# Attention into two expert layers on one core: query tiles by token halves, a rank for each operation of a pair in the scheduler, and constant matmuls over the whole array

## The chip, the cores and the metric

One Trainium2 (trn2) chip, one of its cores. The metric is the device time of one execution in microseconds. The kernel before was timed three times: 1214.74 us median, 1212.67 to 1214.76 us. Engines are called as the profile calls them: PE (TensorE), DVE (VectorE), ACT (ScalarE), POOL (GpSimd), SP (the engine that issues the DMAs). PEld is PE's weight load.

## The reference, cut to what matters

Two batches of 8 heads, 576 tokens, head size 64. Each head adds two attentions: one over keys and values averaged in groups of 4 tokens (144 x 144), its rows repeated 4 times, and one in which a token sees only the keys less than 4 places away. The result, 1152 tokens by 512, goes through two layers of experts (8 and 4 experts, hidden size 1024), each expert computed for every token and weighted.

```python
out_d = sm_attn(q_d, k_d, v_d)              # q_d, k_d, v_d: means over 4 tokens
out_up = np.repeat(out_d, factor, axis=2)   # factor = 4
mask = np.abs(pos[:, None] - pos[None, :]) < factor
scores = np.where(mask, scale * q @ k.T, -1e9)
out_local = softmax(scores) @ v
x = out_up + out_local
for e in range(E):                          # E = 8, then the same with E = 4
    h = np.maximum(x @ w1[e], 0.0)
    out += P[:, e:e + 1] * (h @ w2[e])
```

## The kernel before, in words

**Pairs of heads.** The attention runs over 8 pairs of heads (the loop over `i` at the end of the first plan). A pair fills the partitions: one head on 0 to 63, the other on 64 to 127. For the local attention the 576 queries are cut into 10 tiles of 58 (`QT`; the last has 54), each against a window of 64 keys (`win`). `scores` (L578) computes them in two halves of 5 tiles: a mask matmul (L587), then 10 small matmuls (L594). DVE takes the maximum (L605) and subtracts it (L607), ACT takes the exponential (L612), `norm` sums and inverts on DVE and multiplies on POOL (L622) into `pn`. `pool_qk` and `pool_v` form the averages on POOL; `pooled` (L660) gives the 144 x 144 scores `ed`, which POOL (L686) and ACT (L691) normalise.

**Turning and values.** `turn_scores` (L695) transposes on PE: four blocks of `pn` (L704), then the fifth block and `ed` (L713). Two neighbouring tiles `2t, 2t+1` go through one transpose, so after it the even tiles lie on partitions 0 to 63 and the odd ones on 64 to 127. `values` multiplies them with the values (L749, 20 matmuls) into two banks, one for the even and one for the odd tiles, and the averaged values (L739) into the first. ACT repeats each averaged row 4 times into `od` (L757, 128x576); DVE adds both (L764), taking every second tile of `xs` in each of its two calls. `halves` splits `xs` into two parts `xh` and `xl` (L776, L778), which the expert layers multiply separately.

**What follows.** When the pairs 0 to 3 are done, the tokens of batch 0 are complete, and 8 `plain_unit`s of 12 matmuls (L263) for expert 0 can run beside the pairs 4 to 7. Four tiles of its second product follow (L441, 48 matmuls of 512 columns). Then comes a second plan: gate logits (L901), the same for batch 1, sums of `xh` and `xl` (`x_sums`: POOL L850, DVE L855 and L867), and the expert loop, whose matmuls are L382 and L441.

**The order.** A planner (`Plan`) decides it when the program is built. Each task has an engine, a cost in ns, and a due time, which is PE's planned clock when the task was added plus `slack` plus `bias`. `run` takes the tasks in simulated time: on each engine, of the first `LOOK` tasks by due time, the one that can begin first by the planned costs, ties going to the earlier due time. The result is a fixed list for each engine, so an instruction that waits holds up everything behind it on its engine. Buffers come from rings (`r_pn` has 2, PE's result banks 8).

**Constant matmuls.** `warm_up` (L495) issues matmuls of constants into a free bank, whose result nobody reads: 28 at the start, 12 after the first scores, and up to 16 wherever the planner sees PE idle for over 0.3 us. They load one column of ones (128x1) and stream 128 columns.

```python
    def warm_up(b, n):
        for _ in range(n):
            nc.tensor.matmul(out=b[0:1, 384:512], lhsT=one, rhs=row)
```

Of the kernel before, what the change touches and what calls it, by code (L numbers as in the profile page):

```python
# [78 lines left out]
class Plan:  # L79
# [7 lines left out]
    def __init__(self):  # L87
        self.tasks, self.last, self.readers = [], {}, {}
        self.clock, self.later, self.bias = 0.0, [], 0.0

    def add(self, eng, cost, fn, reads=(), writes=(), slack=0.0, after=None):
# [98 lines left out]
def tile_attention_moe_moe(  # L190
# [22 lines left out]
    QT = W - 6  # L213
    NQ = -(-S // QT)
    SD = S // 4
    HD = SD // 2
# [266 lines left out]
    r_sm, r_ed = ring(4, "sm", [128, NQ, W + 1]), ring(4, "ed", [HD, 4, SD + 1])  # L483
    r_pn = ring(2, "pn", [128, NQ, W])
# [7 lines left out]
    one = nc.const_aps.tensor(1.0, [128, 1], BF16)  # L492
    row = nc.const_aps.tensor(1.0, [128, 128], BF16)

    def warm_up(b, n):  # L495

        for _ in range(n):
            nc.tensor.matmul(out=b[0:1, 384:512], lhsT=one, rhs=row)  # L498

    def win(t):  # L500
        return min(max(QT * t - 3, 0), S - W)

    def queries(t):
        return min(QT, S - QT * t)

# [7 lines left out]
    for j, t in enumerate((0, 1, NQ - 1)):  # L513
        off = win(t) - QT * t

# [12 lines left out]
    for mx in r_mxd.slots:  # L528
        nc.vector.memset(mx[:, :, 1], -scale / 16.0)
    for od in r_od.slots:  # L530
        nc.vector.memset(od[:, S:], 0.0)
    nc.vector.tensor_copy(out=mask[:, 0, :], in_=mask_f[:, 0, :])
# [45 lines left out]
    def scores(i):  # L578

        s = st[i]  # L580
        for h, (lo, hi) in enumerate(HALVES):
# [3 lines left out]
            def mm(lo=lo, hi=hi, n=n, ps=ps):  # L585
# [5 lines left out]
                for t in range(lo, hi):  # L591
                    for y in range(2):
                        p0 = 64 * y
                        nc.tensor.matmul(  # L594
                            out=ps.slot[p0:p0 + queries(t), (t - lo) * W:(t - lo + 1) * W],
                            lhsT=x[p0:p0 + 64, 0, QT * t:QT * t + queries(t)],
                            rhs=x[p0:p0 + 64, 1, win(t):win(t) + W],
                            start=False, stop=(t == hi - 1),
                        )
# [15 lines left out]
    def norm(i):  # L615
# [6 lines left out]
        plan.add("POOL", 1300.0, lambda: nc.gpsimd.tensor_tensor(  # L622
            out=s["pn"].slot, in0=s["sm"].slot[:, :, 0:W],
            in1=s["su"].slot[:, 0:NQ].unsqueeze(2).to_broadcast([128, NQ, W]), op=ALU.mult), (su, *sm), (s["pn"],))

# [69 lines left out]
    def turn_scores(i):  # L695

        s = st[i]
        for j, (lo, hi, x) in enumerate(((0, 4, None), (4, 5, 0), (5, 5, 1))):
            ps = r_bank.new()
            n = 128 * (hi - lo)  # L700

            def mm(ps=ps, lo=lo, hi=hi, x=x, n=n):
                for t in range(lo, hi):
                    nc.tensor.transpose(  # L704
                        ps.slot[:, (t - lo) * 128:(t - lo + 1) * 128],
                        s["pn"].slot[:, 2 * t:2 * t + 2, :].rearrange("p t w -> p (t w)"), ident,
                    )
# [10 lines left out]
            keys = ((s["pn"],) if n else ()) + (((s["ed"], 2 * x), (s["ed"], 2 * x + 1)) if x is not None else ())  # L718
            plan.add("PE", 0.9 * n + (260 if x is not None else 0) + 80, mm, keys, (ps,))
            if n:  # L720
# [8 lines left out]
    def values(i):  # L729
        s = st[i]  # L730

        o = [r_bank.new() for _ in range(2)]
        E = NQ // 2 * QT

        def pooled_values():
            for kt in range(2):
                for x in range(2):
                    p0 = 64 * x
                    nc.tensor.matmul(  # L739
                        out=o[0].slot[p0:p0 + 64, E:E + SD], lhsT=s["vd"].slot[:, 2 * kt + x, :],  # L740
                        rhs=s["adT"].slot[:, x, kt, :], start=(kt == 0), stop=(kt == 1),
                    )

        def local(lo, hi):
            for t in range(lo, hi):
                for x in range(2):
                    for e in range(2):
                        p0, e0 = 64 * x, 64 * e
                        nc.tensor.matmul(  # L749
                            out=o[e].slot[p0:p0 + 64, QT * t:QT * t + QT],  # L750
                            lhsT=s["vw"].slot[e0:e0 + 64, t, p0:p0 + 64],
                            rhs=s["aT"].slot[e0:e0 + 64, t, p0:p0 + QT],
                        )

        plan.add("PE", 600.0, pooled_values, (s["vd"], (s["adT"], 0), (s["adT"], 1)), ((o[0], "d"),))

        plan.add("ACT", 650.0, lambda: nc.scalar.activation(  # L757
            out=s["od"].slot[:, 0:S].rearrange("p (t r) -> p t r", r=4),
            in_=o[0].slot[:, E:E + SD].unsqueeze(2).to_broadcast([128, SD, 4]),
            func=ACTF.Copy, scale=0.25), ((o[0], "d"),), (s["od"],))  # L760
        plan.add("PE", 16 * 60.0, lambda: local(0, 4), (s["vw"], (s["aT"], 0)), ((o[0], "l"), (o[1], "l")))
        plan.add("PE", 4 * 60.0, lambda: local(4, NQ // 2), (s["vw"], (s["aT"], 1)), ((o[0], "l"), (o[1], "l")))
        for e in range(2):
            plan.add("DVE", 170 + E, lambda e=e: nc.vector.tensor_tensor(  # L764
                out=s["xs"].slot.rearrange("p (t e q) -> p t e q", e=2, q=QT)[:, :, e],
                in0=o[e].slot[:, 0:E].rearrange("p (t q) -> p t q", q=QT),
                in1=s["od"].slot.rearrange("p (t e q) -> p t e q", e=2, q=QT)[:, :, e],
                op=ALU.add), ((o[e], "l"), s["od"]), ((s["xs"], e),))

    def halves(i):  # L770
# [6 lines left out]
                 xs, (("xh", i),))  # L777
        plan.add("DVE", 850.0, lambda: nc.vector.tensor_tensor(  # L778
            out=lo, in0=s["xs"].slot[:, 0:S], in1=hi.bitcast(F32), op=ALU.subtract),
# [5 lines left out]
    def warm(n):  # L785
        ps = r_bank.new()
        plan.add("PE", 60.0 * n, lambda: warm_up(ps.slot, n), (), (ps,))

    for i in range(NPAIR):
        pool_qk(i)  # L790
        scores(i)
# [6 lines left out]
        values(i)  # L798
        halves(i)

        if i == HP - 1:
# [272 lines left out]
def _layout(inputs):  # L1074
# [14 lines left out]
    for t in range(NQ):  # L1089
        s = min(max(QT * t - 3, 0), S - W)  # L1090
        vw[:, t % 2, :, t // 2] = vp[:, :, s:s + W].transpose(0, 2, 1, 3)
    v4 = vp.reshape(P, 2, 2, 72, 4, D).transpose(0, 3, 2, 1, 4, 5)
# [48 lines left out]
```

## Time and profile before

| | us |
|---|---|
| median of 3 timed runs | 1214.74 |
| the profiled execution, whole | 1222.66 |
| its span | 1220.9 |
| PE busy | 1213.9 (99%) |
| POOL busy | 679.5 (56%) |
| DVE busy | 665.0 (54%) |
| ACT busy | 463.4 (38%) |

The profiled execution is 7.92 us (0.65%) longer than the median. A stretch of the trace is named by its start and end in us from the span's start. The TensorE clock has two levels, 1.2 and 2.4 GHz; a granted clock of 0.50 is the lower, 1.00 the upper. Attention lies in the first 81 us, the four tiles of L441 behind it end at 91.92, where the logits begin.

### The profile page before, as it was taken

The numbers are of one execution on the slowest core, as the hardware profiler recorded it, in microseconds if no ns is written. First come the engines' busy times: TensorE is split into PE (matmuls) and PEld (weight loads), VectorE is DVE, ScalarE is ACT, GpSimd is POOL, SyncE is SP. The second block draws the span as 40 slices with busy tenths as digits, with TensorE's granted clock in tenths as the row PEclk, the third lists the DMA queues.
The fourth block names the chain that finished last, engine by engine and source line by source line (L and its number), as shares of the span: only waits on it lengthen the run. The fifth ranks groups of instructions, "written<-read, shape, count | busy, mean of one in ns | idle before, by whom it ended". The sixth has DMA issues, their size and how long they took to land.

```text
span 1220.9 us, 20041 instructions
## 1 busy us (share of the span) xinstructions
PE 1213.9 (99%) x7757; PEld 1088.3 (89%) x7757; DVE 665.0 (54%) x1202; ACT 463.4 (38%) x1155; POOL 679.5 (56%) x779
## 2 busy tenths in 40 slices
PE   9999999999999999999999999999999999999998
PEld 7788988989989989989889889899898898898997
DVE  7678846536536446446356356367453563653643
ACT  5565543513414414325325235144452251351430
POOL 7768835736637537438448357266383583573620
PEclk8699999999999999999999999999999999999999
DMA  8420201201202102102111112011021121120102
GB/s 239 127 78 10 96 35 36 69 26 45 69 1 70 53 18 69 45 26 70 38 33 70 35 35 70 32 56 35 18 70 35 35 70 35 36 69 20 34 1 77
DMA packets 27343, 63.71 MB, mean 52 GB/s; under 512 B 4528, under 2 KB 5296, under 8 KB 27248
## 3 DMA queue, kind: packets, MB, share of 16 engines
q1 hardware_dynamic: 27248, 62.44, 16.0%
q8 instruction: 60, 0.98, 0.3%
q14 instruction: 35, 0.29, 0.1%
HBM read 60.07 MB, written 2.36 MB: 51 GB/s over the span
## 4 chain that ended last, share of the span: by engine, by line
PE 96%; DVE 2%; DMA 1%; POOL 1%; issue 0%; ACT 0%; SPq 0%; POOLq 0%; DVEq 0%
PE bank L441 49%; PE bank L382 39%; PE bank L263 4%; PE bank L594 1%; DMA v<-in_v_dram 1%; PE bank L498 1%; PE bank L739 0%; PE bank L749 0%; PE bank L704 0%; DVE ht L352 0%; PE bank L901 0%; PE bank L713 0%; PE bank L877 0%; DVE tmp L392 0%; PE bank L587 0%
## 5 line engine op out<-in xcount | busy, mean ns | idle before, releaser
L441 PE MATMUL bank<-w2s,ht 128*128 128x512 f32 (+1 forms) x2604 | 602.8, 392 | 0.0
L441 PEld LDWEIGHTS bank<-w2s,ht 128*128 128x128 f32 x2604 | 485.1, 188 | 105.9
L289 POOL TENSOR_TENSOR w2s<-raw,w2s 128x512 fp32r<-128x512 f32 x96 | 133.2, 1399 | 396.5 <-PE bank L441 359.9
L469 DVE SCALAR_TENSOR_TENSOR acc<-bank,prob,acc 128x512 f32<-128x512 f32 (+1 forms) x190 | 142.2, 748 | 332.1 <-PE bank L441 332.1
L382 PE MATMUL bank<-sh,w1s 128*128 128x288 f32 x1408 | 294.3, 295 | 0.3 <-DVE tmp L392 0.3
L382 PEld LDWEIGHTS bank<-sh,w1s 128*128 128x128 f32 x1408 | 230.7, 188 | 0.5 <-DVE tmp L392 0.5
L382 PE MATMUL bank<-xh,w1s 128*128 128x288 f32 x1056 | 228.2, 295 | 0.1
L392 DVE TENSOR_TENSOR tmp<-bank,tmp 128x288 f32<-128x288 f32 x352 | 153.2, 450 | 119.2 <-ACT w1s L287 91.7
L352 DVE SCALAR_TENSOR_TENSOR ht<-tmp,ht 128x288 fp32r<-128x288 f32 x264 | 212.4, 831 | 4.4 <-ACT ht L350 1.3
L382 PE MATMUL bank<-sl,w1s 128*128 128x288 f32 x704 | 207.7, 295 | 0.0
L287 ACT ACTIVATE w2s<-raw 128x512 fp32r<-128x512 f32 x96 | 59.7, 624 | 378.8 <-PE bank L441 372.6
L382 PEld LDWEIGHTS bank<-xh,w1s 128*128 128x128 f32 x1056 | 175.6, 188 | 1.2 <-DVE tmp L392 0.4
L382 PE MATMUL bank<-xl,w1s 128*128 128x288 f32 x528 | 156.0, 295 | 0.0
L289 POOL TENSOR_TENSOR w1s<-t,w1s 128x256 fp32r<-128x256 f32 x176 | 141.7, 806 | 12.6 <-PE bank L382 6.6
L350 ACT ACTIVATE ht<-tmp 128x288 fp32r<-128x288 f32 x264 | 111.8, 444 | 88.5 <-DVE tmp L392 87.5
L289 POOL TENSOR_TENSOR w1s<-raw,w1s 128x256 fp32r<-128x256 f32 x148 | 120.5, 815 | 34.7 <-ACT w1s L287 33.7
L382 PEld LDWEIGHTS bank<-sl,w1s 128*128 128x128 f32 x704 | 132.2, 188 | 0.0
L382 PEld LDWEIGHTS bank<-xl,w1s 128*128 128x128 f32 x528 | 99.1, 188 | 0.9
L280 ACT ACTIVATE tmp<-bank 128x288 f32<-128x288 f32 x176 | 69.9, 408 | 64.2 <-PE bank L382 60.6
L352 DVE SCALAR_TENSOR_TENSOR ht<-bank,ht 128x288 fp32r<-128x288 f32 x120 | 54.4, 456 | 52.4 <-ACT ht L350 52.0
L313 POOL TENSOR_TENSOR t<-raw,t 128x256 f32<-128x256 f32 x88 | 80.8, 919 | 3.1
L287 ACT ACTIVATE w1s<-t 128x256 fp32r<-128x256 f32 x176 | 72.1, 410 | 17.8 <-POOL t L313 16.3
(113 smaller groups left out, 862.7 us busy)
## 6 DMA issues: line engine op xcount, KB each, us to landing
raw<-in_w1a_dram SPq DMA_DIRECT2D x32, 512.0 KB, 3.4
raw<-in_w2a_dram SPq DMA_DIRECT2D x64, 256.0 KB, 3.5
raw<-in_w1b_dram SPq DMA_DIRECT2D x16, 512.0 KB, 3.5
raw<-in_w2b_dram SPq DMA_DIRECT2D x32, 256.0 KB, 3.6
qk<-in_qk_dram SPq DMA_DIRECT2D x7, 576.0 KB, 6.3
vw<-in_vw_dram SPq DMA_DIRECT2D x8, 320.0 KB, 7.0
v<-in_v_dram SPq DMA_DIRECT2D x8, 288.0 KB
out_dram<-acc SPq DMA_DIRECT2D x8, 256.0 KB, 2.0
```

Of the source, the lines that this page charges most:

```text
L263: nc.tensor.matmul(out=ps[:, 0:U], lhsT=w[:, j, a:a + 128], rhs=b[:, k, c:c + U], start=(k == 0 and p == 0), stop=(k == HP - 1 and p == 2),)
L280: nc.scalar.activation(out=dst(), in_=src(), func=ACTF.Copy, **kw)
L287: plan.add("ACT", copy_cost(n), lambda: nc.scalar.activation(out=b.slot[:, 0], in_=src(), func=ACTF.Copy), (key,), ((b, 0),))
L289: plan.add("POOL", pool_cost(n), lambda: nc.gpsimd.tensor_tensor(out=b.slot[:, 1], in0=src(), in1=b.slot[:, 0].bitcast(F32), op=ALU.subtract),
L313: plan.add("POOL", pool_cost(256), lambda: nc.gpsimd.tensor_tensor(out=t.slot, in0=x(), in1=y(), op=ALU.subtract), (kx, ky), (t,))
L350: plan.add("ACT", c0[0], lambda: nc.scalar.activation(out=ht[:, s, 0, c:c + U], in_=src(), func=ACTF.Relu), (key,), ((*k, 0),))
L352: plan.add("DVE", c0[1], lambda: nc.vector.scalar_tensor_tensor(out=ht[:, s, 1, c:c + U], in0=src(), scalar=0.0, in1=ht[:, s, 0, c:c + U]. ...
L382: nc.tensor.matmul(out=o, lhsT=w.slot[:, j, 128 * k:128 * k + 128], rhs=a, start=(first and k == 0 and n == 0), stop=(k == 1 and n == 2), ...
L392: plan.add("DVE", cost, lambda: nc.vector.tensor_tensor(out=dst.slot, in0=ps.slot[:, 0:U], in1=b.slot, op=ALU.add), (ps, b), (dst,))
L441: nc.tensor.matmul(out=ps.slot[:, 0:nd], lhsT=ht[:, j, a, 128 * n:128 * n + 128], rhs=w[j].slot[:, b, c0:c0 + nd], start=(j == 0 and p == ...
L469: plan.add("DVE", 130 + 1.2 * nd, lambda: nc.vector.scalar_tensor_tensor(out=a, in0=ps.slot[:, 0:nd], scalar=prob[:, n, e:e + 1], in1=a, o ...
L498: nc.tensor.matmul(out=b[0:1, 384:512], lhsT=one, rhs=row)
```

## The change

1. **Tiles by halves of the tokens.** Tile `t` now begins at `288*(t // 5) + 58*(t % 5)`: five tiles in the first 288 tokens (58, 58, 58, 58, 56), five in the second. One transpose takes tile `j` of both halves, so the even/odd banks of `values` become first half and second half; `xs` is written in one piece for each, and the averaged rows are no longer repeated by ACT (`od` is 128x144) but read four times by DVE's add. Counts of instructions stay the same; one 54-query tile becomes two of 56. The layout of `vw` follows, done before the kernel.
2. **Ranks.** Each of the 42 operations that a pair adds gets its own offset (-37.8 to +30.0 us) on its due time, the same for all 8 pairs. The planner's cost for `xl` rises from 850 to 1200 ns, that for `od` falls from 650 to 300.
3. **Constants over the whole array.** `warm_up` now loads 128x128 ones, and six such matmuls stand at the head of each of the two `pn` transposes of the pairs 0 to 4 (60 in all). The planner sees less idle time on PE, so that of the constants that it fills in itself (16 at the start, then 16, 9 and 8) only the first 16 remain.

```diff
     def add(self, eng, cost, fn, reads=(), writes=(), slack=0.0, after=None):
         n = len(self.tasks)
+        if self.step is not None:
+            slack += self.ranks[self.step]
+            self.step += 1
...
-    r_od, r_xs = ring(2, "od", [128, NQ * QT]), ring(2, "xs", [128, NQ * QT])
+    r_od, r_xs = ring(2, "od", [128, SD]), ring(2, "xs", [128, S])
...
-            nc.tensor.matmul(out=b[0:1, 384:512], lhsT=one, rhs=row)
+            nc.tensor.matmul(out=b[:, 0:128], lhsT=row, rhs=row)
...
+    def begin(t):
+        return U * (t // NJ) + QT * (t % NJ)
...
-            out=s["pn"].slot, in0=s["sm"].slot[:, :, 0:W],
+            out=s["pn"].slot.rearrange("p j e w -> p e j w"),
+            in0=s["sm"].slot[:, :, 0:W].rearrange("p (e j) w -> p e j w", e=2),
...
+            w = 6 if i <= HP and j < 2 else 0
-            def mm(ps=ps, lo=lo, hi=hi, x=x, n=n):
+            def mm(ps=ps, lo=lo, hi=hi, x=x, n=n, w=w):
+                warm_up(ps.slot, w)
                 for t in range(lo, hi):
                     nc.tensor.transpose(
...
-        plan.add("ACT", 650.0, lambda: nc.scalar.activation(
-            out=s["od"].slot[:, 0:S].rearrange("p (t r) -> p t r", r=4),
-            in_=o[0].slot[:, E:E + SD].unsqueeze(2).to_broadcast([128, SD, 4]),
-            func=ACTF.Copy, scale=0.25), ((o[0], "d"),), (s["od"],))
+        plan.add("ACT", 300.0, lambda: nc.scalar.activation(
+            out=s["od"].slot, in_=o[0].slot[:, U:U + SD], func=ACTF.Copy, scale=0.25), ((o[0], "d"),), (s["od"],))
...
-                out=s["xs"].slot.rearrange("p (t e q) -> p t e q", e=2, q=QT)[:, :, e],
+                out=s["xs"].slot[:, U * e:U * e + U].rearrange("p (t r) -> p t r", r=4),
...
+                in1=s["od"].slot[:, HD * e:HD * e + HD].unsqueeze(2).to_broadcast([128, HD, 4]),
...
+    plan.ranks = (
+        25700, 9600, 7500, -3500, -7100, 13600, 100, -12900, 6100, 19200, -2100, 3100,
...
     for i in range(NPAIR):
+        plan.step = 0
         pool_qk(i)
```

Two places on PE show what the ranks do. The first is PE behind the first transposes of pair 1 (`pn_133`, `ed_129`), up to the turn of that pair's `ed`. In the kernel before, 16 matmuls of values (of which two stand here) lie ahead of it:

```order
206 L594 MATMUL bank_104<-qk_110 58x64 x10
207 L749 MATMUL bank_101<-aT_142,vw_114 64x58
208 L749 MATMUL bank_99<-aT_142,vw_114 64x58
...
223 L704 MATMUL bank_105<-ident,pn_133 128x128
224 L713 MATMUL bank_105<-ident,ed_129 72x72 x4
225 L713 MATMUL bank_106<-ident,ed_129 72x72 x4
```

and in the changed kernel (its lines are numbered a little higher: L594 is the mask, L601 the scores, L503 the constants, L717 and L726 the transposes):

```order
214 L717 MATMUL bank_104<-ident,pn_133 128x128 x4
215 L594 LDWEIGHTS twice
216 L594 MATMUL bank_101<-mask,twice 128x320
217 L601 MATMUL bank_101<-qk_111 58x64 x8
...
222 L601 MATMUL bank_100<-qk_110 56x64 x2
223 L503 LDWEIGHTS const-bfloat16-1.0
224 L503 MATMUL bank_105<-const-bfloat16-1.0 128x128
...
235 L717 MATMUL bank_105<-ident,pn_133 128x128
236 L726 MATMUL bank_105<-ident,ed_129 72x72 x4
```

Two halves of scores and six constants now lie between the two turns of pair 1, and the values of that pair come after both.

The second place is PE at the end of attention: the last turn (`ed_131` is that of pair 7), plain units, and the four tiles of L441. In the kernel before:

```order
521 L713 MATMUL bank_106<-ident,ed_131 72x72 x4
522 L263 MATMUL bank_104<-xh,w1s_86 128x288
...
532 L739 MATMUL bank_101<-adT_143,vd_123 64x144 x4
533 L749 MATMUL bank_101<-aT_142,vw_114 64x58
...
537 L263 MATMUL bank_100<-xh,w1s_86 128x288
...
547 L441 MATMUL bank_105<-w2s_88,ht 128x512 x3
...
563 L901 MATMUL bank_99<-xh,wg_a 16x288
```

and in the changed kernel (L447 is the former L441, L751 the averaged values, L761 the values, L922 the logits):

```order
568 L447 MATMUL bank_105<-w2s_91,ht 128x512 x3
569 L761 MATMUL bank_102<-aT_142,vw_113 64x58
...
589 L447 MATMUL bank_101<-w2s_88,ht 128x512 x3
...
595 L726 MATMUL bank_103<-ident,ed_131 72x72 x4
596 L447 MATMUL bank_106<-w2s_88,ht 128x512 x3
...
600 L751 MATMUL bank_102<-adT_143,vd_123 64x144 x4
601 L761 MATMUL bank_102<-aT_142,vw_114 64x58
...
621 L447 MATMUL bank_104<-w2s_88,ht 128x512 x3
...
625 L922 MATMUL bank_99<-xh,wg_a 16x288
```

The tiles of L441 are spread between the turns and values of the pairs 6 and 7, two of them behind the last turn (24 matmuls), and the plain units all stand ahead of them.

## Rows read from the trace of the kernel before

**Rows 1.** The page: the span, and the clock granted to PE in 40 slices.
```profile
span 1220.9 us, 20041 instructions
...
PEclk8699999999999999999999999999999999999999
```

**Rows 2.** Windows: length; busy us of PE, PEld, DVE, ACT, POOL; clock; DMA; GB/s.
```profile
6.43:23.03 16.60, 15.21 (x309) 11.71 (x309) 14.14 (x36) 9.71 (x26) 13.11 (x15) 1.00 0.96 271
23.03:53.75 30.72, 30.72 (x359) 23.35 (x357) 20.48 (x46) 15.22 (x40) 23.58 (x25) 0.50 0.49 137
53.75:81.03 27.28, 26.13 (x359) 22.99 (x358) 17.37 (x38) 21.55 (x58) 19.73 (x23) 1.00 0.31 101
81.03:91.92 10.89, 10.89 (x50) 8.92 (x49) 9.64 (x18) 2.75 (x5) 6.89 (x8) 1.00 0.29 98
```
**Rows 3.** Windows, the same columns, just ahead of the fall of the clock.
```profile
17.00:20.00 3.00, 3.00 (x97) 2.42 (x101) 2.90 (x8) 2.45 (x6) 1.68 (x2) 1.00 1.01 263
20.00:23.00 3.00, 1.92 (x44) 1.29 (x35) 2.05 (x7) 1.73 (x6) 2.84 (x5) 1.00 0.77 189
```

**Rows 4.** Waits of PE in 0 to 160 us: total, times, longest.
```profile
PE bank L713 <- POOL ed L686: 2.0, 2, 1.0
```

**Rows 5.** Timeline of PE at clock 1.00: start, us, instructions.
```profile
7.38 0.31 PE L587 MATMUL bank<-mask,twice 58*128 58x320 bf16 x1
...
8.33 0.31 PE L587 MATMUL bank<-mask,twice 58*128 58x320 bf16 x1
...
57.50 0.60 PE L704 MATMUL bank<-ident,pn 128*128 128x128 f32 x4
58.03 0.71 PE L660 MATMUL bank<-qkd 64*72 64x144 f32 x8
...
61.08 1.05 PE L749 MATMUL bank<-aT,vw 64*64 64x58 f32 x40
62.06 0.71 PE L739 MATMUL bank<-adT,vd 72*64 72x144 f32 x8
62.70 0.81 PE L660 MATMUL bank<-qkd 64*72 64x144 f32 x8
```

**Rows 6.** Timeline of PE at clock 0.50, the same kinds of work.
```profile
25.19 1.23 PE L739 MATMUL bank<-adT,vd 72*64 72x144 f32 x8
26.35 1.12 PE L704 MATMUL bank<-ident,pn 128*128 128x128 f32 x4
27.39 0.44 PE L587 MATMUL bank<-mask,twice 58*128 58x320 bf16 x1
...
29.02 0.44 PE L587 MATMUL bank<-mask,twice 58*128 58x320 bf16 x1
...
33.64 1.34 PE L749 MATMUL bank<-aT,vw 64*64 64x58 f32 x40
34.91 0.44 PE L587 MATMUL bank<-mask,twice 58*128 58x320 bf16 x1
```

**Rows 7.** Timeline of PE: constant matmuls, and what follows the second group.
```profile
14.41 1.08 PE L498 MATMUL bank<-const-bfloat16-1.0 128*1 128x128 bf16 x16
...
52.31 1.12 PE L498 MATMUL bank<-const-bfloat16-1.0 128*1 128x128 bf16 x9
53.35 0.59 PE L713 MATMUL bank<-ident,ed 72*72 72x72 f32 x4
```

**Rows 8.** Timeline of POOL: its last operation of the attention.
```profile
75.38 0.67 POOL L686 TENSOR_TENSOR ed<-ed,su 72x288 f32<-72x288 f32 x1
```

**Rows 9.** Timeline of DVE: last `xl` of the attention, last sums.
```profile
81.72 0.76 DVE L778 TENSOR_TENSOR xl<-xs,xh 128x576 fp32r<-128x576 f32 x1 [0.75 <-ACT xh L776]
...
118.43 3.76 DVE L867 TENSOR_TENSOR sl<-tmp,sh 128x288 fp32r<-128x288 f32 x4
```

**Rows 10.** Timeline of PE: the first two products that use L382.
```profile
124.18 0.30 PE L382 MATMUL bank<-xh,w1s 128*128 128x288 f32 x1
124.32 0.29 PE L382 MATMUL bank<-xl,w1s 128*128 128x288 f32 x1
```

More of the change, by code (lines that the diff above doesn't have):

```diff
@@ L214, in tile_attention_moe_moe @@
     NQ = -(-S // QT)
+    NJ = NQ // 2
     SD = S // 4
@@ L490, in tile_attention_moe_moe @@
     twice = at.tile([QT, 2, 64], BF16, name="twice")
-    one = nc.const_aps.tensor(1.0, [128, 1], BF16)
     row = nc.const_aps.tensor(1.0, [128, 128], BF16)
@@ L497, in warm_up @@
         for _ in range(n):
-            nc.tensor.matmul(out=b[0:1, 384:512], lhsT=one, rhs=row)
+            nc.tensor.matmul(out=b[:, 0:128], lhsT=row, rhs=row)
+    def begin(t):
+        return U * (t // NJ) + QT * (t % NJ)
     def win(t):
-        return min(max(QT * t - 3, 0), S - W)
+        return min(max(begin(t) - 3, 0), S - W)
     def queries(t):
-        return min(QT, S - QT * t)
+        return min(QT, U - QT * (t % NJ))
     warm_up(banks[7], 28)
@@ L513, in tile_attention_moe_moe @@
     for j, t in enumerate((0, 1, NQ - 1)):
-        off = win(t) - QT * t
+        off = win(t) - begin(t)
         for sg in (1, -1):
@@ L595, in mm @@
                             out=ps.slot[p0:p0 + queries(t), (t - lo) * W:(t - lo + 1) * W],
-                            lhsT=x[p0:p0 + 64, 0, QT * t:QT * t + queries(t)],
+                            lhsT=x[p0:p0 + 64, 0, begin(t):begin(t) + queries(t)],
                             rhs=x[p0:p0 + 64, 1, win(t):win(t) + W],
@@ L718, in turn_scores @@
             keys = ((s["pn"],) if n else ()) + (((s["ed"], 2 * x), (s["ed"], 2 * x + 1)) if x is not None else ())
-            plan.add("PE", 0.9 * n + (260 if x is not None else 0) + 80, mm, keys, (ps,))
+            plan.add("PE", 56.0 * w + 0.9 * n + (260 if x is not None else 0) + 80, mm, keys, (ps,))
             if n:
@@ L739, in pooled_values @@
                     nc.tensor.matmul(
-                        out=o[0].slot[p0:p0 + 64, E:E + SD], lhsT=s["vd"].slot[:, 2 * kt + x, :],
+                        out=o[0].slot[p0:p0 + 64, U:U + SD], lhsT=s["vd"].slot[:, 2 * kt + x, :],
                         rhs=s["adT"].slot[:, x, kt, :], start=(kt == 0), stop=(kt == 1),
@@ L763, in values @@
         for e in range(2):
-            plan.add("DVE", 170 + E, lambda e=e: nc.vector.tensor_tensor(
-                out=s["xs"].slot.rearrange("p (t e q) -> p t e q", e=2, q=QT)[:, :, e],
-                in0=o[e].slot[:, 0:E].rearrange("p (t q) -> p t q", q=QT),
-                in1=s["od"].slot.rearrange("p (t e q) -> p t e q", e=2, q=QT)[:, :, e],
+            plan.add("DVE", 170.0 + U, lambda e=e: nc.vector.tensor_tensor(
+                out=s["xs"].slot[:, U * e:U * e + U].rearrange("p (t r) -> p t r", r=4),
+                in0=o[e].slot[:, 0:U].rearrange("p (t r) -> p t r", r=4),
+                in1=s["od"].slot[:, HD * e:HD * e + HD].unsqueeze(2).to_broadcast([128, HD, 4]),
                 op=ALU.add), ((o[e], "l"), s["od"]), ((s["xs"], e),))
@@ L777, in halves @@
                  xs, (("xh", i),))
-        plan.add("DVE", 850.0, lambda: nc.vector.tensor_tensor(
+        plan.add("DVE", 1200.0, lambda: nc.vector.tensor_tensor(
             out=lo, in0=s["xs"].slot[:, 0:S], in1=hi.bitcast(F32), op=ALU.subtract),
@@ L786, in warm @@
         ps = r_bank.new()
+        step, plan.step = plan.step, None
         plan.add("PE", 60.0 * n, lambda: warm_up(ps.slot, n), (), (ps,))
+        plan.step = step
+    plan.ranks = (
[4 rows of a table added]
+    )
     for i in range(NPAIR):
+        plan.step = 0
         pool_qk(i)
@@ L799, in tile_attention_moe_moe @@
         halves(i)
+        plan.step = None
         if i == HP - 1:
@@ L1089, in _layout @@
     for t in range(NQ):
-        s = min(max(QT * t - 3, 0), S - W)
-        vw[:, t % 2, :, t // 2] = vp[:, :, s:s + W].transpose(0, 2, 1, 3)
+        e, j = divmod(t, NQ // 2)
+        s = min(max(S // 2 * e + QT * j - 3, 0), S - W)
+        vw[:, e, :, j] = vp[:, :, s:s + W].transpose(0, 2, 1, 3)
     v4 = vp.reshape(P, 2, 2, 72, 4, D).transpose(0, 3, 2, 1, 4, 5)
```

17 lines of the change are left out of this document (8 added, 9 removed), and 3 rows, old and new, of the table ps.

## The prediction

> **What bounds the kernel now.** I read the page first: a span of 1220.9 us, and a clock of PE that is below full only in the first two of 40 slices [rows 1]. So the one place where much can be won or lost is the front. The windows were cut where the clock changes [rows 2]. From 6.43, where the first scores begin, to 23.03 the clock is 1.00; from 23.03 to 53.75 it is 0.50 and PE is busy in all 30.72 us; from then on it is 1.00. In the slow stretch PE is the bound: DVE is busy 20.48 and POOL 23.58 of the 30.72 us. Behind it PE is busy 26.13 of 27.28 us, then all of 10.89 us in the four tiles of L441. The expert loop behind that is bound by PE at the full clock, and the change leaves its work alone. The time after is therefore decided by the moment L at which the logits begin, 91.92 before.
>
> What went ahead of the fall: in the 3 us from 17 to 20 PE was busy throughout, in the next three 1.92 us [rows 3]. PE's waits name POOL's `ed` (L686), 2.0 us in two waits, the longest 1.0 [rows 4]. In a fixed list, PE stood at the turn of `ed` while the scores behind it could have run.
>
> **What the slow clock costs.** From the start of one item to the start of the next, at full clock: half a pair's scores 0.95 us, four transposes of `pn` 0.53, a pair's values 0.98, its averaged values 0.64 [rows 5]. At half: 1.63, 1.04, 1.27 and 1.16 [rows 6]. With two halves of scores a pair needs 4.05 against 6.73 us in these kinds, a ratio of 0.60. Less the nine constants of 1.04 us [rows 7], the stretch holds 29.7 us of work, worth 17.9 us at full clock: 11.8 us are lost there.
>
> **The change part by part.**
>
> *Constants.* Sixty are added, and the 16, 9 and 8 inside the attention go; those at the start stay 56. A constant costs 0.068 us at full clock (16 in 1.08 us) and 0.116 at half (9 in 1.04) [rows 7]. The trace shows no 128-column load of ones; the bounds are 0.068 and the 0.133 of a 128x128 transpose (0.53 for four [rows 5]). I take 0.068, the row with the same 128 moving columns: +4.1 us, less 1.6 for the 24 that ran at full clock. At the other bound it would be 3.9 us more, were every one uncovered. They stand ahead of transposes that wait for `pn`, so part of them fills waits; I count none as hidden.
>
> *Clock.* What could keep it up is that PE has no holes such as that from 20 to 23 us [rows 3]. The order changes just that: two halves of scores (1.9 us) and six constants lie ahead of the turn of pair 1's `ed`, which waited about 1 us [rows 4]. And should the clock fall, every pair up to the fifth has twelve constants and five transposes close together; nine constants behind four transposes were what ran right before the clock rose at 53.75 [rows 2, 7]. I take the clock as full from 6.43 on.
>
> Here a rule of the Trainium skill bears on the change. The trace shows PE 100% busy over 30.72 us at 0.50 [rows 2]. The page "TensorE: Matmul & The Clock Gate", Part 1, says that the gate goes by how busy PE has been, and that sustained activity releases it. By that rule the stretch should have ended soon, and constants could add nothing, since PE was busy anyway; the trace disagrees: busy time alone does not tell when the clock comes back. I go by the trace; what the rule would do here is the third rival.
>
> *Halved tiles.* The counts of matmuls stay, 58 and 54 queries become 58 and 56: nothing. ACT's `od` has a quarter of the elements, which shortens the way to `xs`; I count no gain, since the values of other pairs lie beside it. DVE's two adds read 288 elements instead of 290, POOL's product writes the same 640 elements in another order: nothing either, with DVE busy 52 of the 74.6 us from 6.43 to 81.03 [rows 2] as the cover. Were POOL's product half as long again (it is one of six operations of a pair on POOL), the cover is that of POOL below.
>
> *L441 moved.* The four tiles (10.89 us [rows 2]) now fill PE between the turns and values of the pairs 6 and 7. Their work is unchanged; it covers waits that PE had there. Late next is POOL's `ed` of pair 7, behind which PE still has 24 matmuls of L441 (half of 10.89), values (0.98) and averaged values (0.64) [rows 5] and a turn, taken as 0.7, so L cannot come earlier than 7.8 us after it. In the kernel before it ended at 76.05 [rows 8]. POOL's own work from 6.43 to there is 13.11 + 23.58 and at most 19.73 us [rows 2], 56.4; without any wait it would end at 62.8, and with POOL idle 15% of the time, near the 21% and 12% that it was idle in the two stages at full clock, at 72.8. That allows L from 80.6 on: near the bound, not over it.
>
> *SP and the loads.* The order of the DMAs is the same; DMA share falls from 0.96 to 0.49 between the first two windows [rows 2], so faster pairs find room.
>
> **The sum.** PE's work from 6.43 to L, at full clock: 15.21 + 17.9 + 26.13 + 10.89 = 70.1; less 1.6, plus 4.1 = 72.6 us. Without a wait L is 79.0. In the two stages at full clock PE waited 1.39 of 16.60 and 1.15 of 27.28 us [rows 2], together 5.8%; at that rate 72.6 us of work take 77.1, and L is 83.5, 8.4 us earlier than 91.92. With no waits the gain is 12.9; with twice as many, 4.
>
> Behind L something is given back. The last `xl` ended at 82.48, the last of the sums that the expert loop needs at 122.19, 39.7 us later [rows 9]. PE came to its first L382 at 124.18, 32.3 us after L [rows 10]. The changed order lets the last `xl` end about when the logits begin, so DVE's 39.7 us now start there, and PE is at L382 32.3 us later. The sums of the first half of the tokens are ready sooner, and the products that need only those, 54 matmuls of 0.14 us [rows 10], last 7.5 us: 39.8 against 39.7. Between nothing and 3 us; I take 0.4.
>
> The change is -8.4 + 0.4 = -8.0 us: the profiled execution of 1222.66 would become 1214.7. It stands 7.9 us over the median of the timed runs. Taking the same difference from the median, I forecast 1214.74 - 8.0 = **1206.7 us**, with a range of its own from 1202 to 1211.
>
> **The rivals.**
>
> 1. *The clock falls again, for part of the time.* DVE was busy 85% and POOL 79% of the time from 6.43 to 23.03 [rows 2]; with PE fast again, PE must wait for them somewhere, and a hole like that of rows 3 may come back. Each us at half clock loses 0.40 us; 10 us of it give -4, so 1210.7. Against it: more constants and fewer holes in the list. 15%.
> 2. *The timed runs do not have the slow stretch.* The profiled execution is 7.9 us longer than their median, close to what the stretch costs; then the profile shows a loss that the timed runs don't have, and the new order and constants change little: 1213 to 1216, 1214.5. Against it: three timed runs agree within 2.1 us, where a clock that falls in some runs and not in others would scatter them. 13%.
> 3. *Slower: the clock falls as before, and constants do not raise it.* PE was busy all through the stretch, and by the Trainium skill's rule above the constants would change nothing there. Then PE is the bound and the constants are added work: 36 of the 60 belong to the pairs 2 to 4, which lie in the stretch, 9 fall away, so 27 at 0.116 [rows 7] are +3.1 us; the 24 of the pairs 0 and 1 replace the 24 removed. 1217.8. It decides from the point where a hole like that of rows 3 remains in the first pairs and nothing brings the clock back before the plain units. For it: the clock fell right behind such a hole [rows 3]. Against it: the rise at 53.75 directly behind constants. 9%.
>
> My forecast keeps 63%.
>
> **How the numbers follow.** About 0.2%, 2.4 us, is what a measurement of this kernel can tell from no change: faster is below 1212.3, slower above 1217.2. The forecast and the first rival are faster, with a little of the second: 0.79. Most of the second and a part of the third are within: 0.13. Slower: 0.08. The range runs from 1202 (gain of 12.7, PE without waits) to 1215.5, which takes in the first rival and most of the second; the third, the top of the second and a few per cent below 1202 are left out.
>
> **What would show it.** Right: a clock of 1.00 from some 6 us on without a break; the plain units some 8 us earlier, the logits near 83.5, and from there on the old pace. Rival 1 would show one or two windows at 0.50 of under 10 us each; rival 2 a trace that gains 8 us and timed runs that don't; rival 3 a stretch at 0.50 as long as before, with constants of 0.116 us in it. If PE waits for DVE's L867 (the sums) at the first products that read them, the give-back was larger than 0.4. The forecast is wrong from the bottom up if L does not move, or if it moves and the span does not.

## The result, and the profile after

The changed kernel takes **1229.05 us** (median of 4 executions, 1227.97 to 1232.71) against 1214.75 of the kernel before beside it (4 executions, 1212.67 to 1224.92): a ratio of 1.0109, 95% interval 1.0076 to 1.0142. It is slower by 14.3 us, where 8.0 us faster was forecast; the range ended at 1215.5. Its profiled execution took 1232.71 us.

The page of the changed kernel, its span and the clock granted to PE in 40 slices, against [rows 1]:

```profile
span 1230.9 us, 20096 instructions
...
PEclk7988999999999999999999999999999999999999
```

The clock is not full throughout. The windows of the changed kernel are cut where the clock changes (columns as in [rows 2]):

```profile
6.43:17.85 11.42, 8.15 (x152) 6.04 (x150) 10.07 (x25) 4.63 (x11) 7.90 (x9) 1.00 1.00 271
17.85:31.50 13.65, 13.65 (x186) 11.33 (x190) 6.40 (x15) 6.29 (x19) 10.02 (x11) 0.50 0.61 173
31.50:62.23 30.73, 27.82 (x478) 23.80 (x471) 29.02 (x52) 22.08 (x61) 28.32 (x31) 1.00 0.50 159
62.23:72.47 10.24, 6.61 (x67) 5.60 (x68) 7.68 (x14) 2.97 (x8) 4.39 (x5) 0.50 0.32 102
72.47:94.89 22.42, 22.03 (x214) 18.05 (x212) 8.11 (x22) 11.27 (x29) 5.96 (x9) 1.00 0.01 1
94.89:106.60 11.71, 8.56 (x66) 6.82 (x65) 7.26 (x16) 4.81 (x12) 11.71 (x15) 1.00 0.25 90
106.60:113.43 6.83, 5.97 (x24) 5.68 (x25) 5.95 (x13) 1.80 (x6) 6.83 (x8) 0.50 0.16 42
```

Three stretches at 0.50, 13.65, 10.24 and 6.83 us long, where before had one of 30.72. The logits begin at 94.89, not at 83.5, and 91.92 before. PE's waits in 0 to 160 us have three entries over 3 us (total, times, longest), where before had none over 2.0 [rows 4]:

```profile
PE bank L751 <- DVE sm L614: 6.0, 1, 6.0
PE bank L998 <- DVE gm L993: 3.6, 1, 3.6
PE bank L601 <- DMA qk<-in_qk_dram: 3.3, 2, 2.6
```

Each of the three has one long wait in it, called a hole from here on (the last entry is two waits, 2.6 us the longer). A stretch at 0.50 begins right behind the hole at 15 us, and during the other two.

**Hole 1, at 15 us, 2.6 us.** The ranks put pair 3's scores ahead of pair 0's second turn. SP issues that pair's `qk` at 7.73, the DMA share is 1.00 up to 17.85 (first window above), and PE stands until it has landed. Timeline of PE:

```profile
14.82 0.31 PE L594 MATMUL bank<-mask,twice 58*128 58x320 bf16 x1
17.75 1.24 PE L601 MATMUL bank<-qk 64*58 64x64 f32 x20 [2.62 <-DMA qk<-in_qk_dram]
18.92 0.82 PE L503 MATMUL bank<-const-bfloat16-1.0 128*128 128x128 bf16 x6
```

**Hole 2, at 59 us, 6.0 us.** Pair 4's `xl` on DVE takes 9.20 us, where 8 of them took 8.1 us together in the kernel before. `sm`, which stands behind it on DVE, must read the bank that PE wants for the averaged values. Timelines of DVE, PE and POOL:

```profile
55.72 9.20 DVE L788 TENSOR_TENSOR xl<-xs,xh 128x576 fp32r<-128x576 f32 x1
64.84 0.48 DVE L614 TENSOR_TENSOR sm<-bank,mx 128x320 f32<-128x320 f32 x1
...
58.88 0.60 PE L717 MATMUL bank<-ident,pn 128*128 128x128 f32 x4
65.47 0.95 PE L751 MATMUL bank<-adT,vd 72*64 72x144 f32 x5 [5.99 <-DVE sm L614]
...
55.52 0.66 POOL L695 TENSOR_TENSOR ed<-ed,su 72x288 f32<-72x288 f32 x1
56.15 1.14 POOL L644 TENSOR_TENSOR t<-qk 128x576 f32<-128x576 f32 x1
...
59.70 0.66 POOL L646 TENSOR_TENSOR qkd<-t 128x288 f32<-128x288 f32 x1
60.33 2.76 POOL L295 TENSOR_TENSOR w1s<-raw,w1s 128x256 fp32r<-128x256 f32 x4
63.05 2.99 POOL L295 TENSOR_TENSOR w2s<-raw,w2s 128x512 fp32r<-128x512 f32 x2
```

All the while POOL runs one instruction behind the other, each on operands in SBUF as `xl`'s are. From the `ed` beside which `xl` begins to the end of the row they are eleven.

**Hole 3, at 104 us, 3.6 us.** Since the tiles of L447 (formerly L441) now lie between the turns, the last `xl` comes at 93.75, when PE is all but at the logits. POOL's first sums begin at 94.65; in the kernel before they began at 82.61, over 9 us ahead of the logits. POOL comes late to `t`, ACT's `w1s` waits for `t`, `ht` stands behind it on ACT, DVE waits for `ht`, and the gate's maximum (`gm`, which PE turns at L998) stands behind that. Timelines of POOL, ACT, DVE and PE:

```profile
94.65 6.88 POOL L871 TENSOR_TENSOR tmp<-xh,xl 128x288 f32<-128x288 f32 x8 [8.43 <-issue]
101.49 1.43 POOL L319 TENSOR_TENSOR t<-raw 128x256 f32<-128x256 f32 x1
...
102.95 0.42 ACT L293 ACTIVATE w1s<-t 128x256 fp32r<-128x256 f32 x1 [2.60 <-POOL t L319]
...
105.91 0.46 DVE L358 SCALAR_TENSOR_TENSOR ht<-bank,ht 128x288 fp32r<-128x288 f32 x1 [3.58 <-ACT ht L356]
...
107.46 0.37 PE L998 MATMUL bank<-ident,gm 128*1 128x128 f32 x1 [3.60 <-DVE gm L993]
```

### The profile page after: what moved, and what is told of

The parts are those of the page before. It is cut to its first block, busy times and chain, and to the rows that moved or that the text cites. A ratio compares the mean times of both kernels' runs of the same rounds, so it can differ in the third digit from the quotient of the medians.

```text
span 1230.9 us, 20096 instructions
## 1 busy us (share of the span) xinstructions
PE 1211.9 (98%) x7784; PEld 1088.5 (88%) x7784; DVE 671.6 (55%) x1200; ACT 462.3 (38%) x1155; POOL 678.4 (55%) x779
## 4 chain that ended last, share of the span: by engine, by line
PE 94%; DVE 3%; DMA 1%; POOL 1%; issue 0%; ACT 0%; DVEq 0%; SPq 0%
PE bank L447 48%; PE bank L388 39%; PE bank L269 4%; DVE xl L788 1%; DMA qk<-in_qk_dram 1%; PE bank L503 1%; POOL tmp L871 1%; PE bank L761 1%; PE bank L601 0%; PE bank L751 0%; DVE ht L358 0%; PE bank L898 0%; DVE sm L614 0%; DVE su L625 0%; PE bank L726 0%
## 5 line engine op out<-in xcount | busy, mean ns | idle before, releaser
L447 PE MATMUL bank<-w2s,ht 128*128 128x512 f32 (+1 forms) x2604 | 604.0, 392 | 0.0
L447 PEld LDWEIGHTS bank<-w2s,ht 128*128 128x128 f32 x2604 | 484.8, 188 | 106.0 <-issue 0.2
L413 POOL TENSOR_TENSOR tmp<-tmp,tmp 128x288 f32<-128x288 f32 x88 | 74.2, 862 | 9.4 <-ACT tmp L286 9.2
```

The lines of the kernel that those rows point to most:

```text
L413: plan.add("POOL", pool_cost(U), lambda u=u: nc.gpsimd.tensor_tensor(out=p5[u].slot, in0=p5[u].slot, in1=p1[u].slot, op=ALU.add), (p1[u], ...
L447: nc.tensor.matmul(out=ps.slot[:, 0:nd], lhsT=ht[:, j, a, 128 * n:128 * n + 128], rhs=w[j].slot[:, b, c0:c0 + nd], start=(j == 0 and p == ...
```

## The experiments

Each run has the kernel before beside it; "over" is the difference of the two medians, since the kernel before itself stood between 1214.2 and 1215.8. The changed kernel is 14.3 over. The ratios with their intervals are not quotients of these medians, and can differ from "over" by up to 2 us: for the changed kernel 1.0109 is 13.2 us.

**1. Whole-array constants alone.** The kernel before with the new constant and nothing else.

```diff
-            nc.tensor.matmul(out=b[0:1, 384:512], lhsT=one, rhs=row)
+            nc.tensor.matmul(out=b[:, 0:128], lhsT=row, rhs=row)
```

> The kernel before, with its 89 constant matmuls over the whole array instead of one column, in the same order. Theory A: nothing of note, within 2 us of the kernel before, with the same slow stretch in the profile. Rival C (whole-array constants are dear): slower by over 3 us, with constants of over 0.1 us at full clock. Rival D (whole-array constants keep the clock up): faster by 3 us or more in the profiled run.

1215.86 us (10 executions), ratio 1.0015 (0.9994 to 1.0036): no effect to be measured. Nor did the form of the constants keep the clock up here: 3 of the 10 executions had a mean clock of 0.999 or more, and 11 of 14 of the kernel before beside them. But the profiled execution was one whose clock stayed full, and it shows how the old order runs when the clock does not fall. The page, one window from the first scores to the logits, and PE's waits:

```profile
span 1211.5 us, 20041 instructions
PEclk9999999999999999999999999999999999999999
...
6.43:82.71 76.28, 70.00 (x1065) 56.84 (x1065) 62.77 (x136) 49.34 (x127) 64.31 (x70) 1.00 0.54 161
...
PE bank L713 <- POOL ed L686: 2.7, 4, 1.3
PE bank L704 <- POOL pn L622: 1.2, 3, 0.5
```

Its logits come at 82.71, 9.2 us ahead of [rows 2], without one instruction in another place. Of 79 timed executions of the kernel before, 38 had a mean granted clock of 0.999 or more (median 1214.0 us), 24 one of 0.995 to 0.998 (1215.7) and 17 one of 0.994 or less (1219.1); the profiled execution that the prediction was read from had 0.987.

**2. Halved tiles alone.** No ranks, no constants at the turns, the old form of constant and the old cost for `xl`.

```diff
-            slack += self.ranks[self.step]
-            w = 6 if i <= HP and j < 2 else 0
+            w = 0
-        plan.add("DVE", 1200.0, lambda: nc.vector.tensor_tensor(
+        plan.add("DVE", 850.0, lambda: nc.vector.tensor_tensor(
```

> The changed tiles alone: tiles by halves of the tokens and the smaller od, with no ranks, the old one-column constants, none at the transposes, and the old planned cost of xl. The planner still makes another order, since od's cost changed. Theory A: no hole of 3 us or more in the front, 1210 to 1217. Rival E (the halved tiles cost the time: DVE's add with the repeated read, POOL's reordered write): the adds take over 0.6 us or the product over 1.6 us each, and the time is 1222 or more.

1218.87 us, ratio 1.0041 (1.0027 to 1.0056), 4.6 over. No hole as long as 1.5 us; the profile is at 0.50 from 20.1 to 33.8 and from 50.8 to 61.1, and none of its five executions had a mean clock over 0.996. The halved tiles do not lengthen an operation (DVE's add 451 ns, before 453; POOL's product 1318 ns in both); this order has its clock lowered oftener than that of before.

**3. The 60 constants not issued**, all else in the same order.

```diff
-                warm_up(ps.slot, w)
```

> The changed kernel without the 60 constant matmuls at the transposes, in the same order (the planner still counts their cost). Theory A (holes of the order): the waits for the loads, for xl and for the gate remain, 12 us of them; at most 4 us of constants go away, most of them hidden, and the clock falls at least as often: 1225 to 1232. Rival C (the constants themselves cost the time): back to 1214 to 1219.

1228.56 us, ratio 1.0129 (1.0073 to 1.0185), 14.3 over: nothing gained. The three holes are there (6.0, 3.0 and 3.6 us), and the first stretch at 0.50 lasts 27.3 us instead of 13.65:

```profile
18.50:45.80 27.30, 26.83 (x341) 21.19 (x341) 15.84 (x36) 14.03 (x40) 20.19 (x24) 0.50 0.63 177
```

The constants are not what makes the changed kernel slow: by the lower end of the interval 8.9 us of the loss are there without them. What they cost by themselves this run does not tell, as its four executions lie between 1221.85 and 1237.53 us.

**4. Hole 2 closed.** POOL copies one column of pair 4's `xl`, so it waits for its end. Nothing else in the order is different.

```diff
+            if i == HP:
+                nc.gpsimd.tensor_copy(out=tiny[:, i:i + 1], in_=lo[:, S - 1:S].bitcast(F32))
```

> The changed kernel with one thing added: behind the subtraction that makes xl of pair 4, POOL copies one column of xl, so POOL cannot begin its next operations before DVE has done xl. The order of all else is that of the changed kernel. Theory A (the order given by the ranks opens holes on PE; the largest, 6.0 us, is there because DVE's xl of pair 4 took 9.20 us while POOL ran operation after operation): xl takes about 1 us, the 6.0 us wait of PE shrinks below 1 us, the fall of the clock behind it goes too, and the time falls by 6 to 9 us against the changed kernel, to 1220 to 1223. Rival B (DVE is late for other reasons, POOL's work is only beside it): xl stays long or the wait comes back elsewhere, and the time stays within 2 us of 1229.

1219.73 us, ratio 1.0053 (1.0034 to 1.0072): 5.5 over instead of 14.3. Timelines of DVE and POOL, and PE's longest waits:

```profile
53.05 2.20 DVE L791 TENSOR_TENSOR xl<-xs,xh 128x576 fp32r<-128x576 f32 x1
...
53.48 1.15 POOL L645 TENSOR_TENSOR t<-qk 128x576 f32<-128x576 f32 x1
55.31 0.19 POOL L793 COPY tiny<-xl 128x1 f32<-128x1 f32 x1 [0.68 <-DVE xl L791]
...
PE bank L1003 <- DVE gm L998: 3.6, 1, 3.6
PE bank L602 <- DMA qk<-in_qk_dram: 2.6, 2, 1.8
```

`xl` is down from 9.20 to 2.20 us, for a wait of POOL of 0.68, and the 6.0 us are gone. The longest wait for `qk`, 1.8 us, is hole 1, shorter here than the 2.6 in the same place of the same order: its length differs from one profile to the next (3.0 us in run 3, 1.5 in run 5, 1.0 in run 6).

**5. The control to it.** The same copy at the same place, but of a column of `xh`, which is ready when `xl` begins.

```diff
-                nc.gpsimd.tensor_copy(out=tiny[:, i:i + 1], in_=lo[:, S - 1:S].bitcast(F32))
+                nc.gpsimd.tensor_copy(out=tiny[:, i:i + 1], in_=hi[:, S - 1:S].bitcast(F32))
```

> As the run that closed pair 4's hole, with the same copy of 128 values on POOL at the same place in the order; only its source is xh, which is ready when xl begins, and not xl, so POOL does not wait for xl's end. Theory A (DVE's xl stands still while POOL issues one instruction on SBUF behind the other): xl of pair 4 takes 6 us or more again, PE waits 4 us or more for DVE's sm behind it, and the time is 1225 to 1232. Rival F (the copy itself, by its place, breaks the row of POOL's instructions or shifts the order's timing, and no wait for xl is needed): xl takes under 3 us and the time is 1218 to 1222.

1228.27 us, ratio 1.0095 (1.0060 to 1.0129), 12.5 over: the hole is back. Timelines of DVE and POOL, PE's longest wait:

```profile
51.95 10.57 DVE L791 TENSOR_TENSOR xl<-xs,xh 128x576 fp32r<-128x576 f32 x1
...
53.48 0.18 POOL L793 COPY tiny<-xh 128x1 f32<-128x1 f32 x1
...
59.42 2.49 POOL L295 TENSOR_TENSOR w2s<-raw,w2s 128x512 fp32r<-128x512 f32 x2
69.50 1.56 POOL L630 TENSOR_TENSOR pn<-sm,su 128x640 f32<-128x640 f32 x1 [7.59 <-DVE su L628]
...
PE bank L752 <- DVE sm L615: 7.3, 1, 7.3
```

`xl` ends at 62.52, 0.6 us after the last instruction of POOL's row (59.42 + 2.49 = 61.91); the next `xl`, which began with POOL at rest, took 0.70 us in all. So it is POOL's instructions, one right behind the other, that `xl` waits for, and the wait of POOL that cured it. Between this run and run 4 lie 7.0 us, and one wait of POOL.

**6. Holes 2 and 3 closed.** As 4, and the tiles of the former L441 planned behind batch 1's `x`.

```diff
-        accumulate(0, n, tile_products(first_w2, n), "copy")
+        accumulate(0, n, tile_products(first_w2, n, after=x_keys(1)), "copy")
```

> Theory A: with pair 4's hole closed and the former tiles of the MoE layer planned behind batch 1's x, the sums on POOL start some microseconds before the logits, the 3.6 us wait at the gate's maximum goes, and the fall of the clock behind it too: 3 to 7 us under 1219.7, so 1213 to 1217; the hole at pair 3's qk (2.6) stays. Rival C (the tiles only change places: the gate's chain is as long as before and PE now has nothing to do while it runs): the wait at the gate's maximum is 2 us or more, 1218 to 1223.

1217.03 us (10 executions), ratio 1.0014 (0.9995 to 1.0032), 2.5 over, 3.0 less than run 4. The entry for `gm` is gone from PE's waits. The 3.0 us are not hole 3 alone, since the planner filled 48 more constants into this order; without these (run 9) it is 4.1 over, 1.4 less than run 4. Of the three for `qk`, hole 1 is 1.01 us here, at pair 3's scores; the longest stands at an earlier pair's:

```profile
PE bank L603 <- DMA qk<-in_qk_dram: 3.3, 3, 1.8
PE bank L728 <- POOL ed L697: 0.8, 2, 0.6
...
18.41 0.78 PE L603 MATMUL bank<-qk 64*58 64x64 f32 x20 [1.01 <-DMA qk<-in_qk_dram]
```

**7. Hole 1: the planner told that pair 3's `qk` lands 3 us later**, so that its scores come behind pair 0's second turn; once with hole 2 closed, once with 2 and 3.

```diff
-                end[i] = wire + 2200.0
+                end[i] = wire + 2200.0 + self.late.get(i, 0.0)
+        if i == 3:
+            plan.late[len(plan.tasks)] = 3000.0
```

> Theory A (three holes of the ranks' order, each with a fall of the clock behind it): with pair 4's hole already closed, pair 3's scores now stand behind pair 0's second turn, so the 2.6 us wait for pair 3's qk goes, and with it the fall of the clock behind it: 1.5 to 5 us under the 1219.7 of the run with pair 4's hole closed alone, so 1214 to 1218; in the profile no wait over 1.5 us for qk before 25 us and no half clock between 6 and 40 us; the wait for the gate's maximum (3.6 us) stays. Rival B (the clock falls for a reason other than the holes, an early stretch being slow as it was in the profiled execution of before): half clock appears between 17 and 40 us without a hole ahead of it, time 1218 to 1222. Rival C (the hole moves: the scores wait the same time at their new place): a wait of 2 us or more for qk at a later point, 1218 to 1221.

> Theory A: all three holes closed at once: no wait over 2 us on PE between 10 and 160 us, full clock from 6 us on, 1209 to 1214, that is at or under before (1214.2), because the order then has the earlier attention which the ranks give and none of their holes. Rival B (the ranks' order costs by itself, whatever its holes): 1215 to 1219, over before, with the waits spread over many short ones.

1220.76 us (ratio 1.0039, 1.0016 to 1.0062), 6.2 over against 5.5 of run 4, and 1219.32 (1.0040, 1.0025 to 1.0056), 4.8 over against 2.5 of run 6. Both miss what the holes' theory expected. In the first the hole moved, much as the last rival had it, if not by the 2 us that it named: PE waits 1.77 us for `qk` at 23.12, where run 4 waited 1.81 at 17.98.

```profile
23.12 1.18 PE L605 MATMUL bank<-qk 64*58 64x64 f32 x20 [1.77 <-DMA qk<-in_qk_dram]
```

Besides, the planner makes another order of all that follows, and in the second sees idle time into which it puts constants, 184 in all where the changed kernel has 116. What hole 1 costs by itself is not settled by this. But six of the seven executions of the second had a mean clock of 0.999 or more, and their median is 1219.0 us, where the kernel before takes 1214.0 at such a clock. So some 5 us are lost here without a fall of the clock, and the profile has no wait over 1.7 us. The 95 more constants than in the kernel before can be behind it (at 0.068 us each they are 6.5 us of work, were none in a wait), or the order itself, as rival B had it; the run does not tell which.

**8. All ranks zero**, halved tiles, constants and planner's costs kept.

```diff
-            slack += self.ranks[self.step]
```

> Theory A: halved tiles, whole-array constants at the turns and the planner's new costs, but all ranks zero: none of the three holes of 2.6, 6.0 and 3.6 us, since each comes from the order that the ranks make; 1213 to 1219, near the run with halved tiles alone (1218.9) and at least 8 us under the changed kernel's 1229. Rival D (the new costs of the planner, not the ranks, make the order with the holes): a hole of 4 us or more in pair 4's neighbourhood and 1224 to 1230.

1215.46 us (10 executions), ratio 1.0007 (0.9995 to 1.0019), 0.9 over: **13.4 of the 14.3 us are the ranks** (by the ratios 12.4 of 13.2). Its clock is full from 6 us on, its logits come at 85.71, and PE's waits are short again:

```profile
6.43:85.71 79.28, 73.04 (x1118) 60.30 (x1116) 64.29 (x136) 46.36 (x127) 64.52 (x70) 1.00 0.53 155
...
PE bank L716 <- POOL pn L628: 2.2, 3, 0.8
PE bank L600 <- DMA qk<-in_qk_dram: 1.5, 1, 1.5
```

**9. What the constants do.** Run 6 without the 48 constants that the planner filled in (116 left), the same without the 60 at the turns as well (56 left), and run 8 without the 60 (77 left instead of 137).

```diff
-    plan.run(idle=lambda b, t: warm_up(b.slot, min(int((t - 100.0) / 60.0), 16)) if t > 300.0 else None)
+    plan.run(idle=fill_once)
```

> The run with pair 4's hole closed and the former tiles put behind batch 1 had 164 constants on PE, since the planner filled 48 into the idle time that it saw; here those 48 are left out (116 remain, as in the changed kernel), all else in the same order. Theory A (a constant is work on PE and costs its 0.068 us wherever no wait covers it): 48 times 0.068 = 3.3 us less than 1217.0, at most half of it hidden, so 1213.7 to 1215.4. Rival E (the fills keep the clock up): stretches of half clock of 10 us or more appear and the time is 1218 to 1224.

> As the run before, and without the 60 constants at the transposes either (56 remain, all before 15 us). Theory A with full clock: another 60 times 0.068 = 4.1 us, partly in waits: 1210 to 1213, under before. Rival E (the constants keep the clock up where PE has waits of 0.5 to 2 us): half clock for 10 to 30 us between 17 and 60 us, so 1217 to 1226. I hold E the likelier here, since without them the changed kernel's clock was low for 27 us at a stretch and not 14.

> The changed kernel with all ranks zero and without the 60 constants at the transposes (77 remain against 137). If they only cost: 1215.5 less 60 times 0.068 = 4.1, so 1211 to 1214. If they keep the clock up: stretches at half clock in the profile, as with the halved tiles alone, and 1217 to 1221. If the two cancel: 1214 to 1217.

> The run with all three holes closed had 184 constants, 68 more than the changed kernel, put in by the planner; here 116. Theory A: 68 times 0.068 = 4.6 us less than 1219.3, so 1213 to 1216 if the clock stays up. Rival E (the fills keep the clock up): half clock for 10 us or more, 1218 to 1224. Rival B (the order of the ranks costs by itself): full clock and still 1217 to 1219.

| run | constants | median us | over | executions with a mean clock of 0.999 or more |
|---|---|---|---|---|
| 6 | 164 | 1217.03 | 2.5 | 6 of 10 |
| 6, not filled | 116 | 1219.79 | 4.1 | 2 of 10 |
| 6, no constant after the start | 56 | 1218.13 | 2.4 | 0 of 10 |
| 8 | 137 | 1215.46 | 0.9 | 7 of 10 |
| 8, none at the turns | 77 | 1217.35 | 1.6 | 2 of 10 |

The second of run 7 without fills (116) took 1222.21 us, 6.5 over; its profile has a wait of 3.6 us for POOL's `ed`, which none of the expectations had. Leaving constants out made no version faster than the one that has them all: with fewer of them PE has less to do, and its clock is down oftener. The intervals of these runs overlap (ratios 1.0014, 1.0027 and 1.0033 for the first three), so the times cannot tell them apart. That the constants keep the clock up is told by the last column, 13 of 20 against 4 of 30. The runs with fewer were timed later and on another chip, but the kernel before beside them was at such a clock about as often (13 of 31) as beside the others (12 of 27). What they cost where the clock is full anyway is seen in two profiles at full clock: PE is busy 73.04 us up to the logits in run 8, with 137 constants, and 70.00 in run 1, with 89 (the 48 more, at 0.068 us each, would be 3.3 us). Run 8 without the 60 has a fall in its profile, in a window with PE busy throughout:

```profile
6.43:21.47 15.04, 12.79 (x247) 9.93 (x250) 12.97 (x32) 8.44 (x23) 11.64 (x13) 1.00 1.02 267
21.47:38.50 17.03, 17.03 (x233) 12.82 (x231) 11.96 (x26) 9.64 (x28) 14.84 (x17) 0.53 0.76 210
```

## Why the prediction was wrong

**The first step that failed: "Taking the same difference from the median".** The slow stretch was in the profiled execution [rows 2], and without it there is something to win: at full clock the old order has its logits at 82.71, which is 9.2 us earlier (run 1), against 11.8 us by the sum. But by their times the three executions that the median came from had no stretch of that length (none took over 1214.76 us), and of 79 later ones only 17 had a mean clock of 0.994 or less. So there was under 1 us of it to win in the median (1214.74 against 1214.0 at full clock). That was the second rival, at 13%; it saw why nothing would be gained, but not that the time would rise. What was held against it, that three timed executions agreed within 2.1 us, speaks for it: none of the three was as long as the profiled one. Had the forecast taken the stretch as absent, the logits at 83.5 would have stood against 82.7, a change of nothing.

**The second, which made the kernel slower: "in the two stages at full clock PE waited ... together 5.8%; at that rate".** An order that ranks make anew has its own waits. The old order at full clock waited 8.2% (76.28 less 70.00 us, run 1), the new one without ranks 7.9% (run 8), but the ranks' order has three single holes of 12.2 us in all. They need looking for one by one: what does PE now come to first, and what is late for it?

- *"SP: the order of the DMAs is the same ... so faster pairs find room."* It is the same, and that is how hole 1 comes about: PE's order moved pair 3's scores ahead, the queue that feeds them did not move. The DMA share of 0.96 in [rows 2] spoke of the full queue.
- *"nothing either, with DVE busy 52 of the 74.6 us ... as the cover".* The cost of DVE was taken as its busy time. Hole 2 (7 to 9 of the 14.3 us, runs 4 and 5) is one DVE instruction that stretched from about 1 to 9.20 us beside a row of POOL's. The row of `xl` in [rows 9] (0.76 us) was one with POOL at rest; the mean of all eight in that kernel, 1011 ns with 1.89 us at the longest, was a hint.
- *"I take 0.4"* for what is given back behind L. The chain of `xl`, sums and L382 was followed, the gate's chain was not: POOL's sums, late now, hold the splits of the weights, and through ACT and DVE the gate's maximum. Closing hole 3 brought 1.4 to 3.0 us (runs 6 and 9), and its wait is 3.6 us, where 0 to 3 were allowed for by another chain.
- *"I take the clock as full from 6.43 on".* It fell three times. Rival 1 had the form of it, one or two windows at 0.50 of under 10 us, but only as something taken off a gain; here there are three, two of them longer, and each came with a hole that the old order does not have.

**What held.** Halved tiles lengthened neither DVE's add nor POOL's product (run 2). A whole-array constant costs what a column's did (16 in 1.10 us in run 1, [rows 7] 1.08). The sum of work on PE, 72.6 us from the first scores to the logits, was near: 73.04 in run 8, with 21 more constants than the changed kernel. And the clock stayed at 0.50 with PE busy throughout, for 30.72 us in [rows 2] and for 13.65 in the changed kernel, and for 27.3 us with PE busy for 26.83 of them (run 3). The Trainium skill, page "TensorE: Matmul & The Clock Gate", Part 1, says that activity releases it; these traces do not bear that out, if activity is what the profile counts as busy. The third rival said that constants bring the clock nothing; run 9 speaks against that.

**The books.** By the medians, 14.3 us over = hole 2 with its fall of the clock 8.8 (run 4), the step of run 6 with hole 3 in it 3.0, what is left of the ranks 1.6 (run 6 against 8; hole 1 is in it, and 27 more constants), and 0.9 that does not differ from nothing (run 8). By the ratios the same four are 6.8, 4.7, 0.9 and 0.9 of 13.2 us. So the total of the ranks is sure and hole 2 the largest part; the split is good to some 2 us, and it depends on the order in which the holes were closed. Hole 1's part was expected to be larger; by this sum it is small, but no run takes it away alone, and the runs that tried (7) got slower, so it stays open. No version here beats the kernel before.

## What to carry to other kernels

A profiled execution that is longer than the timed median, here by 0.65%, may have something in it that the median has not: find that first, and take no gain out of it. When a scheduler's order is changed by weights, the average share of waits of the old order is no guide (5.8% here, and three holes of 12.2 us came); go through the new order for each engine and ask of every piece that moved ahead whether its load, its bank and the other engine's instruction move with it. And where a DVE instruction with two SBUF operands stands ahead of something that PE waits for, look at what POOL has queued beside it: one wait of 0.68 us on POOL was worth 7 to 9 us here (runs 4 and 5).

## What was not expected of the hardware

DVE's `xl` (128x576, both inputs in SBUF) took 0.70 to 0.76 us where it began with POOL at rest, up to 4.4 us beside some of POOL's work (run 6), and 9.20 and 10.57 us beside closed rows of eleven and twelve POOL instructions. It did not get its turn after one of these: in run 5 it ended 0.6 us behind the end of the row, in run 4 as much behind the instruction after which POOL waited. In the changed kernel it got through beside the last of the eleven, which began 0.65 us ahead of `xl`'s end and took 1.78 us, where the one before it, of the same kind, took 1.25:

```profile
64.27 1.78 POOL L295 TENSOR_TENSOR w2s<-raw,w2s 128x512 fp32r<-128x512 f32 x1
```

The Trainium skill, page "SBUF — State Buffer", section "Who interferes with whom", says that a DVE instruction with two SBUF inputs contends with a POOL instruction that reads SBUF, and that the ports which the two share are an exclusive lock. The runs agree. That the waiting side can lose many times in a row, for 10 us, is what they show beyond it; why `xl` got through at one place and not at another stays open.

The clock of PE fell in orders without a hole of 1.5 us too (run 2), and in the kernel before itself it was at 0.999 or more on the mean in 38 of 79 executions and at 0.994 or less in 17. What decides it between two executions of the same kernel stays open.
